# Two more chunk pairs of the first FFN in Strassen's form: the sixth of its third group and the fifth of its fourth

## The chip, the cores and the metric

The kernel runs on one core of one Trainium2 chip. The metric is the device time of one execution in microseconds. The median of three runs of the kernel before is 401.58 us (401.27 to 401.74).

## The reference

Four layers run one after another on one sequence of 2048 rows and 512 features, in bfloat16, each with a layer norm in front and a residual sum behind: linear attention A with 32 heads, gated FFN B with 1792 hidden features, then A and B again with the same weights.

```python
phi = lambda t: jnp.where(t > 0, t + 1, jnp.exp(t)) + 1e-6
kv = jnp.einsum("bhsd,bhse->bhde", phi(k), v)
num = jnp.einsum("bhqd,bhde->bhqe", phi(q), kv)
den = jnp.einsum("bhqd,bhd->bhq", phi(q), z)[..., None] + 1e-6     # z: phi(k) summed over s
A(x) = (num / den) @ wo                                            # q, k, v = x @ wqkv
B(x) = (silu(x @ w_gate) * (x @ w_up)) @ w_down
x = x + A(norm(x));  x = x + B(norm(x));  x = x + A(norm(x));  x = x + B(norm(x))
```

## The kernel before

**Layers and groups.** The layers are numbered 0 (A), 1 (B), 2 (A), 3 (B). The 2048 rows are 16 tiles of 128; the FFN works on four groups (0 to 3) of 512 rows. The 1792 hidden features are 14 chunks of 128 (0 to 13).

**Plain chunk.** A token such as `1u304` (layer 1, group 3, chunk 04) is eight matmuls of 512 columns on TensorE (PE): four with `Wg` into one bank, four with `Wu` into another. ScalarE (ACT) takes the silu of the first (`silu`, line 1013), VectorE (DVE) multiplies by the second and writes the chunk of `hT` (`h`, line 1018). Once layer 2's K and Q tiles have begun, ACT would have to change its table for a silu, so there the chunk is a tanh on ACT (line 1001) and two steps on DVE (`gst` line 1003, `h` line 1009).

**Strassen's form.** A token such as `1y243` (layer 1, group 2, pair 4, product 3) belongs to a family that computes chunks j and j + 7 of a group together. The two chunks, the two halves of the 512 features and the two halves of the group's rows make a 2 x 2 block product, done with seven products (Winograd's form of Strassen's algorithm) in place of eight. One product is four matmuls of 256 columns, two for the gate and two for the up projection, side by side in one bank. Function `gs` (line 1180) issues it and what follows it: products 1, 6 and 7 are copied by ACT into a buffer (`cp`, line 1248); after products 2, 3 and the later of 5 and 7, DVE adds the bank to such a buffer (`ca`, line 1227), ACT takes the silu (`sih`, line 1219), and GpSimd (POOL) or DVE multiplies into `hT` (`hp`, line 1242); after product 4, ACT takes a silu (line 1219) and DVE multiplies (`hh`, line 1258). Some products add into the bank of another one, and may only after that one was copied:

```python
own = FIRST[i]
fresh = own == i
...
assert done.issuperset({2: (1,), 6: (1,), 7: (6,), 4: (7,), 3: (5, 7)}.get(i, ()))
```

**Operands of the families.** Products 3, 5, 6 and 7 read sums of weight blocks (`ws`, line 1101). One piece of sums, `W0`, `W1`, `W2`, `W3`, serves two pairs: `W2` serves pairs 4 and 5. Layer 1 keeps `W2` in the first 4096 columns of the tensor `Wqkv`, whose own contents nobody needs between layers 0 and 2. Most products also read sums of blocks of the rows (`xs`, line 1147), one set for each group; group 3 keeps its set in `Wo`. Before layer 2 the attention's weights are loaded anew by POOL's queue, once all readers of the sums there are done (function `reload`, its loads through the helper `dma`, line 535): `R.ldk` and `R.ldk1` bring the K part in two halves of 256 KB, `R.ldq` and `R.ldv` the Q and V parts of 512 KB each, `R.ldo` brings `Wo`:

```python
for c in range(2):
    dma("pool", Wqkv[:, 2 * c:2 * c + 2, D:2 * D], wq3[:, 2 * c:2 * c + 2, D:2 * D], w=[f"Wk{c}"], kind="ldk")
dma("pool", Wqkv[:, :, 0:D], wq3[:, :, 0:D], w=["Wq"], kind="ldq")
dma("pool", Wqkv[:, :, 2 * D:], wq3[:, :, 2 * D:], w=["Wv"], kind="ldv")
```

**Other tokens.** `2k0` is a K tile of layer 2 (four matmuls of 512 columns, `phi` of it by ACT's exponential, line 700, and DVE), `2q10` a Q tile, `1p25` a piece of the down-projection of layer 1's group 2 (14 matmuls of 256 columns; it too is in Strassen's form).

**What sets the order.** It is written out by hand. The table `PROGRAM` lists the tokens in the order in which PE works; the list `PE_T` holds times that belong to it. The tables `ORDER["act"]`, `["dve"]`, `["pool"]`, `["sp"]` list every operation of the other engines by name (`1y243.hp` is the product of token `1y243`, `2x4.apply` a step of a tile's layer norm). Each engine runs its list in order; waits between engines follow from the buffers that an operation reads and writes. `ON_POOL` and `ON_ACT` hold the names of operations that are placed on another engine than the usual one. All matmuls of the tokens are issued by one helper (line 492).

Of the kernel before, what the change touches and what calls it, by code (L numbers as in the profile page):

```python
# [206 lines left out]
2d22 2d23 2g4 2d11 2d12 2g1 2d13 2q33 2v 2m0 2m1 2m3 2m2 2r1 2w3 2w2 2w0 2w1 2q30 2q32 2w4 2d31 2w6 2w8 2w7 2w10 2d33
2w9 2d30 2d32 2w11 2w5 3U008 3u008 3u001 3u004 3u010 3u000 2w12 3u005 3u009 3u002 2w15 3u012 2w13 3u011 2w14 3u007
3y101 3u003 3y105 3y111 3y106 3y115 3u006 3y116 3y102 3y107 3u013 3y104 3y103 3y121 3y112 3y117 3p01 3p05 3y113 3p06
3y125 3y114 3p02 3y131 3y126 3p07 3y132 3u106 3y136 3y122 3y127 3y137 3p03 3y151 3y124 3y135 3y152 3y156 3u113 3y157  # L210
3y123 3y155 3p04 3y133 3y141 3y154 3y134 3y211 3y145 3y146 3y153 3y255 3y216 3y215 3y147 3y142 3y217 3y212 3y251 3y144
# [1377 lines left out]
```

## Time and profile before

| what | value |
| --- | --- |
| median of three runs | 401.58 us (401.27 to 401.74) |
| the profiled execution | 401.14 us, of which the profile's span is 399.4 us |
| PE busy | 394.3 us, 2922 matmuls |
| DVE, ACT, POOL busy | 327.5, 268.8, 214.5 us |

The profile is one execution. The span is what the profiler sees from the first to the last instruction; 1.74 us of the execution lie around it. Busy time of an engine is the time in which an instruction of it ran; "idle before" gives what an engine waited for. In a timeline row, a start time and a duration stand first, then the engine, the line of the kernel, the operation, what it writes from what it reads, its shape and the number of equal instructions in a row; a duration covers them all, and since matmuls overlap at their ends, the next row's start tells better when the next one began. The names of tensors are those of the allocated buffers: `pk`, `Wqkv` or `Wo` as the operand of a matmul of 256 columns are mostly sums that are kept there.

### The profile page before, as it was taken

What the parts mean: (1) busy time and instruction counts of PE and PEld (TensorE: products, weight loads), DVE (VectorE), ACT (ScalarE), POOL (GpSimd) and SP (SyncE); (2) the same over time, 40 slices, a digit from 0 to 9 for tenths busy, and PEclk for the clock granted to TensorE, in tenths of its full rate; (3) what the DMA queues carried; (4) which work ended last, traced back from release to release, by engine and by line L of the source; (5) the groups of instructions that cost most, each with busy time, mean ns of one, the idle gap of its engine ahead of it and who ended that gap; (6) DMA issues with size and microseconds to landing.
All of it is one profiled execution on the core that took longest, in us unless ns stands there. A gap on an engine that the chain in (4) does not pass through costs nothing.

```text
span 399.4 us, 7922 instructions
## 1 busy us (share of the span) xinstructions
PE 394.3 (99%) x2922; PEld 264.5 (66%) x2922; DVE 327.5 (82%) x785; ACT 268.8 (67%) x569; POOL 214.5 (54%) x352
## 2 busy tenths in 40 slices
PE   7999999999999999999999999999999999999997
PEld 6444555445787787565786445454588888888886
DVE  5996599377987779699997666987698889899997
ACT  5999886763656876668367968695755673886550
POOL 5623254998879799960446503467747260431230
PEclk9999999999999999999999999999999999999999
DMA  8646662540020021721002103323112100100011
GB/s 268 167 91 228 158 158 60 150 121 2 2 42 12 2 41 29 210 50 45 2 16 59 33 15 67 69 53 67 39 28 41 36 19 2 55 0 2 2 53 54
DMA packets 53783, 25.43 MB, mean 64 GB/s; under 512 B 46512, under 2 KB 52144, under 8 KB 53744
## 3 DMA queue, kind: packets, MB, share of 16 engines
q1 hardware_dynamic: 51264, 16.27, 18.4%
q0 software_dynamic: 1936, 8.13, 6.4%
q10 hardware_dynamic: 544, 0.52, 0.4%
q8 instruction: 23, 0.38, 0.4%
q14 instruction: 16, 0.13, 0.1%
HBM read 11.80 MB, written 2.10 MB: 35 GB/s over the span
## 4 chain that ended last, share of the span: by engine, by line
PE 97%; DMA 1%; DVE 1%; ACT 0%; issue 0%; SPq 0%; DVEq 0%
PE pb L492 97%; DMA X<-in_A_x_dram 1%; DVE pq L1442 0%; PE pb L679 0%; ACT xnA L624 0%; ACT xnA L616 0%; DVE stats L609 0%; DVE etmp L809 0%; SPq L535 0%; DVEq L1559 0%; DVE xnA L655 0%; DVE mv L611 0%; DVE vpe L640 0%; DVE xnA L1368 0%
## 5 line engine op out<-in xcount | busy, mean ns | idle before, releaser
L492 PE MATMUL pb<-xnT,Wg 128*128 128x512 bf16 (+1 forms) x332 | 75.3, 334 | 0.0
L492 PE MATMUL pb<-xnT,Wu 128*128 128x512 bf16 (+1 forms) x332 | 75.3, 334 | 0.0
L1242 POOL TENSOR_TENSOR hT<-pq 128x256 bf16<-128x256 f32 x45 | 34.1, 769 | 45.4 <-ACT pq L1219 45.3
L1248 ACT ACTIVATE pq<-pb 128x512 f32<-128x512 f32 x63 | 36.6, 594 | 28.2 <-PE pb L492 24.8
L492 PEld LDWEIGHTS pb<-xnT,Wu 128*128 128x128 bf16 x332 | 32.5, 98 | 24.2
L1227 DVE TENSOR_TENSOR pq<-pb,pq 128x512 f32<-128x512 f32 x63 | 41.9, 682 | 5.7 <-PE pb L492 2.9
L492 PEld LDWEIGHTS pb<-xnT,Wg 128*128 128x128 bf16 x332 | 32.3, 98 | 21.2 <-DMA xnT<-xnB 0.2
L1018 DVE TENSOR_TENSOR hT<-tht,pb 128x512 bf16<-128x512 f32 x46 | 30.8, 681 | 17.2 <-ACT tht L1013 12.2
L644 POOL TENSOR_TENSOR rstd<-vpe,negh 128x1 f32<-128x1 f32 x62 | 36.5, 590 | 9.5 <-DVE vpe L640 7.3
L1013 ACT ACTIVATE tht<-pb 128x512 f32<-128x512 f32 x46 | 26.4, 594 | 22.5 <-PE pb L492 21.5
L492 PE MATMUL pb<-Wd,hT 128*128 128x256 bf16 x336 | 40.3, 273 | 0.0
L700 ACT ACTIVATE etmp<-pb 128x512 bf16<-128x512 f32 x64 | 36.7, 601 | 3.8 <-PE pb L492 2.9
L492 PEld LDWEIGHTS pb<-Wd,hT 128*128 128x128 bf16 x336 | 32.9, 98 | 4.2
L492 PE MATMUL pb<-pk,xnA 128*128 128x512 bf16 (+1 forms) x152 | 34.7, 362 | 0.0
L492 PE MATMUL pb<-xnT,Wqkv 128*128 128x512 bf16 (+1 forms) x132 | 32.8, 376 | 0.0
L705 DVE TENSOR_SCALAR etmp<-etmp 128x512 bf16<-128x512 bf16 x64 | 19.4, 314 | 15.5 <-ACT etmp L700 15.5
L492 PE MATMUL pb<-Wqkv,xnT 128*128 128x512 bf16 x128 | 30.8, 379 | 0.0
L1219 ACT ACTIVATE pq<-pq 128x256 f32<-128x256 f32 x63 | 24.9, 411 | 8.1 <-DVE pq L1227 8.0
L492 PE MATMUL pb<-GT,pq 128*128 128x512 bf16 x128 | 29.9, 379 | 0.0
L624 ACT ACTIVATE etmp<-X,sums 128x512 bf16<-128x512 bf16 x32 | 22.9, 715 | 5.0 <-DVE X L945 3.8
L628 POOL TENSOR_SCALAR mv<-sums 128x1 f32<-128x1 f32 x52 | 14.1, 275 | 21.2 <-DVE X L945 12.5
L945 DVE SCALAR_TENSOR_TENSOR X<-pb,X 128x512 bf16<-128x512 f32 x32 | 21.1, 681 | 3.5 <-PE pb L492 3.4
(218 smaller groups left out, 887.8 us busy)
## 6 DMA issues: line engine op xcount, KB each, us to landing
...
Wd<-in_B_w_down_dram POOLq DMA_DIRECT2D x7, 256.0 KB, 3.3
X<-in_A_x_dram SPq DMA_DIRECT2D x6, 256.0 KB, 4.8
Wqkv<-in_A_wqkv_dram SPq DMA_DIRECT2D x2, 512.0 KB, 7.4
Wo<-in_A_wo_dram POOLq DMA_DIRECT2D x2, 512.0 KB, 4.6
Wqkv<-in_A_wqkv_dram POOLq DMA_DIRECT2D x2, 512.0 KB, 5.1
```

The lines of the kernel that those rows point to most:

```text
L492: return op("pe", lambda e: e.matmul(o_ap, lhsT=lhsT, rhs=rhs, start=start, stop=stop, skip_group_check=skip), r=r, w=w, n=n)
L624: op("act", lambda a: a.activation(out=sq_ap, in_=X[:, t, :], func=ACT.Square, scale=-float(D), bias=sums[:, t:t + 1], accum_out=mv[:, t, ...
L644: op("pool", lambda p: p.tensor_tensor(out=rstd[:, t:t + 1], in0=vpe[:, t:t + 1], in1=negh[:], op=ALU.pow), r=[f"vp{t}", "negh"], w=[f"rs{ ...
L700: exps.append(op("act", lambda a: a.activation(out=etmp[e][:], in_=PB[pb], func=ACT.Exp), r=[f"pb{pb}"], w=[f"e{e}"], after=silus, kind="e ...
L705: op("dve", lambda v: v.tensor_scalar(out=etmp[e][:], in0=etmp[e][:], scalar1=1.0, scalar2=1e-6, op0=ALU.min, op1=ALU.add), r=[f"e{e}"], w ...
L945: op("dve", lambda v: v.scalar_tensor_tensor(out=X[:, t, :], in0=PB[pb], scalar=1.0, in1=X[:, t, :], op0=ALU.mult, op1=ALU.add, accum_out= ...
L1013: silus.append(op("act", lambda e: e.activation(out=tht[a][:], in_=PB[pg], func=ACT.Silu), r=[f"pb{pg}"], w=[f"th{a}"], after=exps, kind=" ...
L1018: op("dve", lambda v: v.tensor_tensor(out=hT[h][:, j, :], in0=tht[a][:], in1=PB[pu], op=ALU.mult), r=[f"pb{pu}", f"th{a}"], w=hk, kind="h")
L1219: silus.append(op("act", lambda e: e.activation(out=o_ap, in_=i_ap, func=ACT.Silu), r=r, w=w, after=exps, kind="sih" if len(w) == 1 else " ...
L1227: op("dve", lambda v: v.tensor_tensor(out=c, in0=PB[b], in1=c, op=ALU.add), r=[f"pb{b}", k], w=[k], kind="ca")
L1242: lambda e: e.tensor_tensor(out=hT[h][:, jj, o:o + 256], in0=c[:, 0:256], in1=c[:, 256:512], op=ALU.mult),
L1248: op("act", lambda e: e.activation(out=c, in_=PB[pb], func=ACT.Copy), r=pk_, w=[k], kind="cp")
```

## The change

Only tables change. Two plain pairs become families: chunks 5 and 12 of group 2 (`1u205`, `1u212`) become `1y251` to `1y257`, chunks 4 and 11 of group 3 (`1u304`, `1u311`) become `1y341` to `1y347`. Pairs 4 and 5 use the sums `W2`, and both groups have their sums of rows for other families, so no operation `ws` or `xs` is new. `PROGRAM` differs in these lines only (and in the wrapping of the lines behind):

```diff
-1u303 1y243 1u212 1u306 1u205 1u309 1y301 1y311 1u302 1y306 1u310 1y316 1y315 1y307 1y305 1u313 1y317 1y304 1y302
-1y312 1y303 1y313 1y314 2k0 2k1 2q10 2k4 1u304 2k3 2k2 2k6 1p21 2q01 2k5 1u305 1p26 1p22 1p27 1p25 1u311 1p24 1u312
+1u303 1y251 1y243 1y252 1y256 1y345 1u306 1y255 1y257 1y341 1u309 1y253 1y301 1y342 1y254 1y346 1y311 1u302 1y306
+1u310 1y347 1y315 1y316 1y344 1y307 1y343 1y305 1u313 1y317 1y304 1y302 1y312 1y303 1y313 1y314 2k0 2k1 2q10 2k4 2k3
+2k2 2k6 1p21 2q01 2k5 1u305 1p26 1p22 1p27 1p25 1p24 1u312 1p23 1p31 1p35 2k7 1p36 1p33 1p37 2k11 2q02 1p34 1p32 2q12
```

`PE_T` gets new numbers. The tables of ACT, DVE, POOL and SP get the operations of the new families in place of those of the four chunks, and in all four layers some neighbours change places. PE has 2946 matmuls in place of 2922, ACT 10 operations more, DVE 2, POOL 6, SP none. `ON_ACT` gets the name `1c303`, which moves nothing: the chunk's product stays on DVE, since the buffer that the other way needs is lent at that point. All lines behind the tables stand three lines lower (L492 becomes L495, L535 becomes L538, L1242 becomes L1245).

The first place is on PE, behind the chunk `1u303`, where layer 1's last chunks and families stand. Before:

```order
L492 MATMUL pb<-xnT,Wg 128x512 x4
L492 MATMUL pb<-xnT,Wu 128x512 x4
L492 MATMUL pb<-xnT,Wqkv 128x256 x4
L492 MATMUL pb<-xnT,Wg 128x512 x4
L492 MATMUL pb<-xnT,Wu 128x512 x4
L492 MATMUL pb<-xnT,Wg 128x512 x4
L492 MATMUL pb<-xnT,Wu 128x512 x4
L492 MATMUL pb<-xnT,Wg 128x512 x4
L492 MATMUL pb<-xnT,Wu 128x512 x4
```

The same place after:

```order
L495 MATMUL pb<-xnT,Wg 128x512 x4
L495 MATMUL pb<-xnT,Wu 128x512 x4
L495 MATMUL pb<-xnT,Wg 128x256 x2
L495 MATMUL pb<-xnT,Wu 128x256 x2
L495 MATMUL pb<-xnT,Wqkv 128x256 x4
L495 MATMUL pb<-xnT,Wg 128x256 x2
L495 MATMUL pb<-xnT,Wu 128x256 x2
L495 MATMUL pb<-pk,Wqkv 128x256 x4
L495 MATMUL pb<-Wo,Wqkv 128x256 x4
L495 MATMUL pb<-xnT,Wg 128x512 x4
L495 MATMUL pb<-xnT,Wu 128x512 x4
```

Behind `1u303` there stood `1y243` (the row with `Wqkv`, the last one there that reads `W2`) and three plain chunks; now there stand `1y251`, `1y243`, `1y252`, `1y256` and `1y345`, and the first plain chunk comes behind them.

The second place is on POOL, around the reload of the attention's weights. Before:

```order
L628 TENSOR_SCALAR mv<-sums 128x1
L1242 TENSOR_TENSOR hT<-pq 128x256
L535 DMA Wqkv<-in_A_wqkv_dram 128x2x512 x2
L628 TENSOR_SCALAR mv<-sums 128x1
L1242 TENSOR_TENSOR hT<-pq 128x256
L535 DMA Wqkv<-in_A_wqkv_dram 128x4x512 x2
L640 TENSOR_SCALAR vpe<-mv 128x1
L1242 TENSOR_TENSOR hT<-rrep 128x256
```

After:

```order
L1245 TENSOR_TENSOR hT<-pq 128x256 x2
L1150 TENSOR_TENSOR Wo<-xnT,Wo 128x512
L1245 TENSOR_TENSOR hT<-pq 128x256
L538 DMA Wqkv<-in_A_wqkv_dram 128x2x512 x2
L538 DMA Wqkv<-in_A_wqkv_dram 128x4x512 x2
L1245 TENSOR_TENSOR hT<-rrep 128x256
L538 DMA Wo<-in_A_wo_dram 128x4x512
L1245 TENSOR_TENSOR hT<-pq 128x256 x5
L1245 TENSOR_TENSOR hT<-GT 128x256
L768 TENSOR_TENSOR GT<-GT,pk 128x512
```

The four loads into `Wqkv` stood ahead of the layer norms of layer 2 (`mv`, `vpe`) and of four operations `xs` and `hp`; now they stand behind the last row sum of group 3 and directly ahead of the last products of layer 1 and of layer 2's first sums of K (`GT<-GT,pk`).

The third place is PE's start of layer 2, from the last two products of layer 1 (`1y313`, `1y314`) to the first piece of the down-projection, `1p21`. Before:

```order
L492 MATMUL pb<-Wo,Wg 128x256 x2
L492 MATMUL pb<-Wo,Wu 128x256 x2
L492 MATMUL pb<-Wqkv,xnT 128x512 x8
L492 MATMUL pb<-xnT,Wqkv 128x512 x4
L492 MATMUL pb<-Wqkv,xnT 128x512 x4
L492 MATMUL pb<-xnT,Wg 128x512 x4
L492 MATMUL pb<-xnT,Wu 128x512 x4
L492 MATMUL pb<-Wqkv,xnT 128x512 x12
L492 MATMUL pb<-Wd,hT 128x256 x14
```

After:

```order
L495 MATMUL pb<-Wo,Wg 128x256 x2
L495 MATMUL pb<-Wo,Wu 128x256 x2
L495 MATMUL pb<-Wqkv,xnT 128x512 x8
L495 MATMUL pb<-xnT,Wqkv 128x512 x4
L495 MATMUL pb<-Wqkv,xnT 128x512 x16
L495 MATMUL pb<-Wd,hT 128x256 x14
```

The chunk `1u304`, which stood between the K tiles `2k4` and `2k3`, is gone from there; its work stands ahead of `2k0` now.

## Rows read from the trace of the kernel before

**Rows 1.** The page: PE's busy time, granted clock by slice, the chain that ended last
```profile
PE 394.3 (99%) x2922; PEld 264.5 (66%) x2922; DVE 327.5 (82%) x785; ACT 268.8 (67%) x569; POOL 214.5 (54%) x352
...
PEclk9999999999999999999999999999999999999999
...
PE 97%; DMA 1%; DVE 1%; ACT 0%; issue 0%; SPq 0%; DVEq 0%
```

**Rows 2.** Waits of PE over the span: us in total, times, longest
```profile
PE pb L492 <- DVE hT L498: 1.2, 1, 1.2
PE pb L679 <- DVE xnA L655: 0.8, 1, 0.8
```

**Rows 3.** Timeline of PE, start and duration in us, from 152 to 194
```profile
152.80 1.04 PE L492 MATMUL pb<-pk,Wqkv 128*128 128x256 bf16 x8
...
154.15 0.39 PE L492 MATMUL pb<-pk,Wg 128*128 128x256 bf16 x2
...
156.13 1.03 PE L492 MATMUL pb<-xnT,Wg 128*128 128x512 bf16 x4
...
157.86 0.60 PE L492 MATMUL pb<-xnT,Wqkv 128*128 128x256 bf16 x4
...
166.07 1.03 PE L492 MATMUL pb<-xnT,Wg 128*128 128x512 bf16 x4
166.94 1.03 PE L492 MATMUL pb<-xnT,Wu 128*128 128x512 bf16 x4
167.80 0.60 PE L492 MATMUL pb<-Wo,pk 128*128 128x256 bf16 x4
...
176.49 1.89 PE L492 MATMUL pb<-Wqkv,xnT 128*128 128x512 bf16 x8
178.22 1.03 PE L492 MATMUL pb<-xnT,Wqkv 128*128 128x512 bf16 x4
...
190.77 3.22 PE L492 MATMUL pb<-Wd,hT 128*128 128x256 bf16 x28
193.83 1.69 PE L492 MATMUL pb<-Td,RT 128*128 128x256 bf16 x14
```

**Rows 4.** The page's groups of a family's side work: busy us, mean ns of one
```profile
L1242 POOL TENSOR_TENSOR hT<-pq 128x256 bf16<-128x256 f32 x45 | 34.1, 769 | 45.4 <-ACT pq L1219 45.3
L1248 ACT ACTIVATE pq<-pb 128x512 f32<-128x512 f32 x63 | 36.6, 594 | 28.2 <-PE pb L492 24.8
...
L1227 DVE TENSOR_TENSOR pq<-pb,pq 128x512 f32<-128x512 f32 x63 | 41.9, 682 | 5.7 <-PE pb L492 2.9
...
L1219 ACT ACTIVATE pq<-pq 128x256 f32<-128x256 f32 x63 | 24.9, 411 | 8.1 <-DVE pq L1227 8.0
```

**Rows 5.** Windows, 156 to 181: busy us of PE, weight loads, DVE, ACT, POOL
```profile
156.00:181.00 25.00, 25.00 (x148) 14.29 (x147) 19.73 (x40) 16.84 (x37) 19.72 (x31) 1.00 0.48 122
```

**Rows 6.** Waits of POOL, 156 to 212: us in total, times, longest
```profile
POOL GT L765 <- DVE pk L709: 11.2, 1, 11.2
```

**Rows 7.** Timeline of ACT: a copy (153.50) and the change of tables
```profile
153.50 0.60 ACT L1248 ACTIVATE rrep<-pb 128x512 f32<-128x512 f32 x1 [1.36 <-PE pb L492]
...
179.49 1.28 ACT L700 ACT_TABLE_LOAD   x1
180.78 0.60 ACT L700 ACTIVATE etmp<-pb 128x512 bf16<-128x512 f32 x1
```

**Rows 8.** Timeline of POOL: the issues of the four loads into `Wqkv`
```profile
158.76 1.53 POOL L535 DMA_DIRECT2D Wqkv<-in_A_wqkv_dram  x2 [0.23 <-PE pb L492]
...
161.18 1.56 POOL L535 DMA_DIRECT2D Wqkv<-in_A_wqkv_dram  x2
```

**Rows 9.** The page's DMA issues: KB each, median us from issue to landing
```profile
Wqkv<-in_A_wqkv_dram SPq DMA_DIRECT2D x2, 512.0 KB, 7.4
...
Wqkv<-in_A_wqkv_dram POOLq DMA_DIRECT2D x2, 512.0 KB, 5.1
...
Wqkv<-in_A_wqkv_dram POOLq DMA_DIRECT2D x2, 256.0 KB, 4.0
```

More of the change, by code (lines that the diff above doesn't have):

```diff
@@ L207 @@
[L207 to L211, printed above, removed]
@@ L218 @@
+3y323 3p27 3y367 3y362 3y333 3y364 3y324 3y363 3y341 3y345 3p24 3y346 3y342 3y334 3y347 3p23 3y344 3y343 3p31 3p32
+3p35 3p36 3p33 3p37 3p34
 """
@@ new lines @@
+0k11.id1 0q02.id1 0q02.exp 0k12.exp 0k12.id1 0q23.exp 0q22.id1 0q22.exp 0d0.ln 0d0.rex1 0d0.rex3 0q21.exp 0q10.id1
+0d0.rex 0q10.exp 0d0.rex2 0q20.exp 0d1.ln 0d1.rex3 i.c1 0d1.rex1 0G2.evac 0G3.evac 0d1.rex 0q30.exp 0d1.rex2 0q31.exp
+0M3.evac 0M0.evac 0M1.evac 0q33.exp 0d2.ln 0d2.rxs 0q33.id1 1x1.sq 1x2.sq 1x3.sq 1x2.apply 0q32.exp 1x0.sq 1x3.apply
+1x4.sq 1x5.sq 1x7.sq 1x6.sq 1x4.apply 1u012.silu 0d3.rep1 1u000.silu 1x9.sq 1x11.sq 1u001.silu 1x7.apply 1u007.silu
+0d3.rep 1u011.silu 1u004.silu 1u005.silu 0d3.rep3 1u006.silu 1u003.silu 1x6.apply 1x10.sq 1u010.silu 0d3.rep2
@@ new lines @@
+1u013.silu 1u002.silu 1y121.cp 1u008.silu 1u113.silu 1x8.sq 1y101.cp 1u009.silu 1u104.silu 1y122.sih 1y126.cp
+1u105.silu 1y106.cp 1x13.sq 1y127.cp 1y107.cp 1y131.cp 1y124.sih 1y136.cp 1x9.apply 1y102.sih 1y104.sih 1y137.cp
+1x12.sq 1y134.sih 1y123.sih 1y105.sih 1u112.silu 1y111.cp 1y116.cp 1x15.sq 1y127.sih 1y132.sih 1y117.cp 1y103.sih
+1y117.sih 1y112.sih 1x14.sq 1y135.sih 1y133.sih 1u111.silu 1y114.sih 1y221.cp 2x2.sq 1u106.silu 2x1.sq 1y226.cp
+1y201.cp 2x3.sq 1y227.cp 1y113.sih 2x0.sq 1u206.silu 1y222.sih 1y227.sih 1u213.silu 1y211.cp 1x13.apply 1y231.cp
@@ new lines @@
+2q31.id1 2q31.exp 2q21.exp 2q20.id1 2q03.exp 2q03.id1 2d0.ln 2d0.rex1 2d0.rex3 2d0.rex 2q13.exp 2d0.rex2 2q23.exp
+2q23.id1 2q22.exp 2q22.id1 2d2.ln 2d2.rex1 2d2.rex 2G2.evac 2G3.evac 2d1.ln 2q33.id1 2d1.rxs 2q33.exp 2M0.evac
+2M1.evac 2M2.evac 2d2.rex3 2d2.rex2 3x3.sq 3x2.sq 2q30.exp 3x0.sq 2q32.exp 3x1.sq 3x0.apply 3x8.sq 3x6.sq 3x4.sq
+3x9.sq 3x7.sq 3x6.apply 3x10.sq 2d3.rep 2d3.rep1 3u008.silu 3u004.silu 3x7.apply 3u010.silu 3u001.silu 2d3.rep2
+2d3.rep3 3u000.silu 3u009.silu 3u005.silu 3x5.sq 3x5.apply 3u012.silu 3x11.sq 3u002.silu 3x12.sq 3x15.sq 3u007.silu
@@ L263 @@
+3y307.sih 3y312.sih 3y357.sih 3y321.cp 3y303.sih 3y313.sih 3y361.cp 3y326.cp 3y336.cp 3y322.sih 3y327.cp 3y337.cp
+3y366.cp 3y332.sih 3y327.sih 3y367.cp 3y335.sih 3y367.sih 3y364.sih 3y324.sih 3y362.sih 3y323.sih 3y333.sih 3y341.cp
+3y363.sih 3y346.cp 3y347.cp 3y334.sih 3y342.sih 3y347.sih 3y344.sih 3y343.sih
 """,
```

265 lines of the change are left out of this document (126 added, 139 removed).

## The prediction

> **What bounds the kernel now.** I read the page first: TensorE (PE) is busy 394.3 of 399.4 us, its clock is granted in full in all 40 slices, and 97% of the chain that ended last is PE's matmul line [rows 1]. The view of PE's waits names little: 1.2 us once for an evacuation, 0.8 us once for a normalised input [rows 2], both far from the stretch that changes (156 to 212 us). PE runs without a hole there, so the kernel's time is the sum of its matmuls, and an edit is worth what it takes out of that sum less the waits that it puts in. Two prices are read from PE's timeline [rows 3]. A plain chunk is 8 matmuls of 512 columns: one ran from 166.07 to 167.80, 1.73 us. A run of 28 matmuls of 256 columns went from 190.77 to 193.83, 3.06 us, and 28 of that size is what one Strassen family of seven products issues.
>
> **What is taken out.** Two plain pairs, four chunks, go: 4 x 1.73 = 6.92 us, less rounding 6.90. Two families come: 2 x 3.06 = 6.12, or 6.10 where the row's own small gaps are left out. PE's sum falls by **0.80 us** (0.40 a pair), although it has 24 matmuls more (32 leave, 56 come). No sum of weights or of rows is added: those of pairs 4 and 5, and of both groups, stand for other families. 0.80 us is 0.2% of 401.58 us, and 0.2% is about what a measurement of this kernel can tell from no change, so the whole gain lies just on that edge.
>
> **Side work.** For each pair the families add to ScalarE (ACT) three copies and four silus, to VectorE (DVE) three sums and one product, to GpSimd (POOL) three products; the plain chunks' silus, tanhs and products go. By count that is ACT +10, DVE +2, POOL +6. From the mean durations of the groups (594, 682, 411 and 769 ns, [rows 4]; a plain chunk's silu and product, of the copy's and the sum's shape, taken at 594 and 682), the stretch before layer 2 gains on ACT 6 x 0.59 + 8 x 0.41 - 2 x 0.59 = 5.6 us, on DVE 6 x 0.68 + 2 x 0.41 - 2 x 0.68 = 3.5 us. It was 25 us long with ACT 16.84, DVE 19.73 and POOL 19.72 busy [rows 5] and becomes 27.65 long: 22.4, 23.2, and POOL up to 24.3. All fit under PE; POOL moreover leaves some of its six products (4.6 us) for the 11.2 us in which it waited for layer 2's first sums [rows 6]. I cost this at nothing as a sum of busy time; what can cost is order, below.
>
> **Copies that a product waits for.** Within a family a later product adds into a bank only after ACT has copied it. Row 152.80 (x8) starts with a seventh product; its copy runs on ACT from 153.50 for 0.60 [rows 7], and the fourth product, which needs it, starts at 154.15, 1.35 us after the seventh began. Three products back to back are 3 x 0.436 = 1.31. So the pattern "product, two other products, dependent one" holds PE for 0.04. The new families have it twice: 1y251, 1y243, 1y252, then 1y256; and 1y347, 1y315 with 1y316, then 1y344. Cost 2 x 0.04 = **0.09 us**; lower end 0; higher end 0.3 each, if ACT comes to the copy after another instruction of half a microsecond.
>
> **The reload of the attention's weights.** This is the part with the least room. The sums of weights for pairs 4 and 5 lie in a part of the QKV weights' own tensor, which POOL reloads once their last reader has run; layer 2's first matmuls read the reloaded tensor. Before, the last reader was 1y243, at 157.86; the first pair of loads started on POOL at 158.76 (0.90 after that), the second at 161.18 [rows 3, 8], and layer 2 began at 176.49, more than 10 us after they had landed. Now the new families read the same sums and the last reader is 1y343, and from its start to layer 2 PE has nine products, itself among them, and one plain chunk: 9 x 0.436 + 1.73 = 5.65 us.
> PE gets two families and loses only two chunks before layer 2 (the other two stood inside layer 2), so layer 2 starts at 176.49 + 6.10 - 3.45 = 179.1, its second half of the first K tile's operands is wanted at 179.5, and the first Q tile (178.22 before) at 180.86. 1y343 starts at 179.1 - 5.65 = 173.5. With the same 0.90, and 1.53/2 = 0.77 per issue on POOL [rows 8]: first K load 174.4, second 175.1, Q load 175.9. Landings by the page: 4.0 us for 256 KB, 5.1 for 512 KB from POOL [rows 9]. So K lands at 178.4 and 179.1 (0.7 and 0.4 us early), Q at 181.0 (0.15 late). The V load is wanted later still. Bounds: the Q load can be 0.15 early-to-late around zero, since it shared the DMA engines before with transposes and now stands in an emptier stretch; the high end is the slowest 512 KB of the page, 7.4 us, from the SP queue at the start [rows 9]. I take **0.08 us**, half of 0.15, since POOL's own rows are the nearest. Queued behind on POOL are the products 1y305.hp to 1y302.hp and the reload of Wo; PE's down-projection is the reader of the former and comes some 6 us later.
> The Trainium skill (DMA: Bandwidth & Descriptors, Anatomy of one DMA, the SWDGE path) states a fit of about 2.0 us plus bytes over 436 GB/s. Worked out from that page as an estimate, 256 KB would land in 2.6 us and 512 KB in 3.2, and the term would be zero with over a microsecond to spare; the rows (4.0 and 5.1) say otherwise here, and the sum goes by them.
>
> **The start of layer 2.** The change takes two chunks out of it: 1u304 stood among the K tiles, 1u311 among the down-projection. There ACT had switched to the table of the exponential (1.28 us from 179.49, first exponential at 180.78, [rows 7]) once its last silu had run. Now more silus stand before that switch, and layer 2 starts 2.65 us later, so I place the switch at about 182.7 and the first exponential at 184.0, 3.2 us after its matmuls ended instead of 2.6. PE goes on with K and Q tiles and a down-projection meanwhile; the first matmul that wants a bank back is 1u305, at about 188.4, and adding up the durations along DVE's order, I find what frees it done about half a microsecond before. In return DVE loses there two gated products of two steps each (2 x 2 x 0.68 = 2.7 us). I take zero; ends -0.2 and +0.8.
>
> **The rest of the tables.** The orders of ACT, DVE, POOL and SP are also permuted a little in all other layers, PE's is not. The waits that PE shows there are 2.2 us in all [rows 2], so a permutation can give at most a few tenths, and can take as much. I take zero, plus or minus 0.2.
>
> **Sum.** -0.80 + 0.09 + 0.08 = -0.63 us. The profiled execution took 401.14 us (span 399.4 and 1.74 around it): it would take 400.51. The median of the runs, 401.58, stands 0.44 above the profiled one, so I give **400.95**.
>
> **Rivals.**
> 1. *The whole gain, or a little more.* Neither thin place costs anything and the permuted tables close some of the tenths that PE waits elsewhere: 401.58 - 0.80 = 400.78, less 0 to 0.5, so 400.3 to 400.78. For it: the landings of before were taken with transposes in the same microseconds, and PE's waits outside the stretch leave something to win. Against it: the copy pattern is a row of before, and nothing was added to hide it.
> 2. *The reload lands late; slower.* One mechanism: layer 2's first K tile waits for the K loads. At the 7.4 us of the SP queue the first lands at 174.4 + 7.4 = 181.8, 2.65 us after PE wants it; the Q load's lateness lies under that. 401.58 - 0.80 + 0.09 + 2.65 = 403.5. It decides from a landing of 4.7 us on, and makes the kernel slower by over 0.2% from about 6.3 us. Against it: POOL's own loads of this size took 4.0 to 5.1.
> 3. *A backlog at the switch of tables.* ACT comes 0.5 to 1 us later to the first exponential than I place it, DVE with it, and PE waits for a bank at 1u305 or for a product at the down-projection: 401.2 to 401.9, no change that could be told; with two such waits 402.5.
> 4. *Matmuls are not priced by columns.* If a matmul of 256 columns cost more than half of one of 512, Strassen's form would lose. At a spacing of 98 ns for 256 columns and 131 for 512, a plain pair is 16 x 0.131 = 2.10 us and a family 28 x 0.098 = 2.74: +0.64 a pair, so 402.9. Those two figures are from the Trainium skill (TensorE: Matmul & The Clock Gate, Back-to-back issue gap), which gives 131 ns at 512 and 81 at 128 for a sustained stream; 98 is my interpolation, an estimate. The trace speaks against the mechanism: 1.73 us for 8 is 216 ns, and 3.06 for 28 is 109, a ratio of 1.98 [rows 3].
>
> **Chances.** My forecast (400.75 to 401.15): 0.42. Rival 1: 0.32. Small stalls of rivals 2 and 3 that leave it within 0.2% of before: 0.14. Rival 2 with the slower ending 0.06, rival 3 with it 0.04, rival 4 0.02. Faster is rival 1 and a sliver of the forecast, 0.35; slower 0.12; the same 0.53. Range 400.2 to 402.2: below lies little of rival 1, above the three slower cases.
>
> **What would show it.** Right: in the stretch from 156 to the start of layer 2 PE runs 2.65 us longer, 1p25 (193.83 before) starts 0.9 later than before, and what follows it, with 1u311 gone, 0.7 earlier; holes of about 0.04 ahead of 1y256 and 1y344. Wrong: a wait of PE for a DMA into the QKV weights, or the K loads landing more than 4.7 us after their issue (rival 2); a wait of the matmuls of 1u305 for DVE (rival 3); 28 products that take more than 3.1 us (rival 4); or PE's waits of 1.2 and 0.8 us elsewhere grown or gone, which the part on the rest of the tables puts at zero.

## The result, and the profile after

The changed kernel is slower: 405.09 us in the median of four runs (404.32 to 405.43), before 401.56 in the same runs. The ratio is 1.0086, with an interval of 1.0070 to 1.0102. The profiled execution took 405.43 us, its span 403.7 (before 401.14 and 399.4): 4.3 us more.

The page of the kernel after, where [rows 1] stood for before (busy time, clock by slice, chain that ended last):

```profile
PE 396.1 (98%) x2946; PEld 267.8 (66%) x2946; DVE 333.7 (83%) x787; ACT 271.9 (67%) x579; POOL 219.5 (54%) x358
...
PEclk9999999899999999999999999999999999999999
...
PE 93%; DVE 3%; issue 2%; DMA 1%; ACT 1%; POOL 0%; DVEq 0%; POOLq 0%
```

PE has 24 matmuls more and, which could not be if only the sum of matmuls had changed, more busy time; one slice, the eighth, has a lower clock; and DVE's share of the chain has risen from 1% to 3%. PE's waits of after, the answer to [rows 2]:

```profile
PE pb L495 <- DVE X L948: 3.0, 1, 3.0
PE pb L495 <- DVE hT L501: 1.2, 1, 1.2
PE pb L495 <- DMA xnT<-xnB: 0.2, 1, 0.2
```

One wait of 3.0 us for a residual sum of layer 0 (line 948) is new; the 0.8 us of before's second line, at the program's start, are not there. PE's timeline of after says where it stands: nearly 90 us ahead of the first matmul that the change touches.

```profile
70.47 1.03 PE L495 MATMUL pb<-xnT,Wu 128*128 128x512 bf16 x4
74.47 1.52 PE L495 MATMUL pb<-xnT,Wg 128*128 128x512 bf16 x4 [2.97 <-DVE X L948]
75.78 1.91 PE L495 MATMUL pb<-xnT,Wu 128*128 128x512 bf16 x4
77.49 1.43 PE L495 MATMUL pb<-xnT,Wg 128*128 128x512 bf16 x4
78.75 1.03 PE L495 MATMUL pb<-xnT,Wu 128*128 128x512 bf16 x4
```

The row at 74.47 is the plain chunk `1u007` of layer 1's first group. Behind the wait four matmuls take 1.71 us (75.78 to 77.49) in place of 0.86. The windows of after (PE, weight loads, DVE, ACT, POOL, then PE's granted clock) show why:

```profile
70.50:74.40 3.90, 1.00 (x5) 0.27 (x3) 3.90 (x4) 3.81 (x9) 3.89 (x4) 1.00 0.17 34
74.40:78.60 4.20, 4.13 (x12) 1.54 (x13) 2.65 (x8) 1.69 (x3) 4.00 (x9) 0.59 0.89 158
78.60:90.00 11.40, 11.40 (x55) 5.16 (x54) 5.52 (x8) 5.55 (x12) 8.36 (x14) 1.00 0.50 138
```

After three idle microseconds PE's granted clock was 0.59 for 4.2 us, most of it at the lower of its two levels (1.2 GHz), then full again. Beside before, PE stands 0.10 us later at the first chunk `1u012`, 3.23 later at `1u007` and 4.93 later at `1u011`: 3.13 for the wait and 1.70 for the clock.

What DVE and POOL did then, in that order:

```profile
67.72 0.95 DVE L887 RECIPROCAL rtok<-dsb 128x128 bf16<-128x128 f32 x1
69.24 4.56 DVE L658 TENSOR_SCALAR xnB<-X,mv,rstd 128x512 bf16<-128x512 bf16 x1 [0.57 <-POOL rstd L647]
73.72 0.68 DVE L948 SCALAR_TENSOR_TENSOR X<-pb,X 128x512 bf16<-128x512 f32 x1
```

```profile
68.63 0.57 POOL L647 TENSOR_TENSOR rstd<-vpe,negh 128x1 f32<-128x1 f32 x1
69.18 2.25 POOL L1104 TENSOR_TENSOR xnA<-Wg 128x512 bf16<-128x512 bf16 x2
71.40 1.14 POOL L1104 TENSOR_TENSOR pk<-Wu 128x512 bf16<-128x512 bf16 x1
72.51 1.14 POOL L1104 TENSOR_TENSOR xnA<-Wu 128x512 bf16<-128x512 bf16 x1
73.60 0.79 POOL L538 DMA_DIRECT2D Wd<-in_B_w_down_dram  x1
```

The DVE row at 69.24 is `1x5.apply`, the last step of a layer norm (tile 5 of layer 1): 0.41 us in the kernel before, here 4.56. It began 0.06 us after POOL began four sums of weights (`ws`) in a row, and ended 0.15 us after the last of them. That it began there is in the order itself: the step waits for `rstd`, and POOL makes `rstd` (68.63) in the instruction directly ahead of the four sums. The residual that PE waits for, `0w8.res`, stands behind the step on DVE. In the kernel before, these names stood in another order: POOL had one sum, then small steps and a DMA issue, and DVE had `0w8.res` seven places ahead of `1x5.apply`. The same step there, and POOL beside it:

```profile
69.68 0.41 DVE L655 TENSOR_SCALAR xnB<-X,mv,rstd 128x512 bf16<-128x512 bf16 x1
```

```profile
68.71 1.15 POOL L1101 TENSOR_TENSOR xnA<-Wg 128x512 bf16<-128x512 bf16 x1
69.83 0.34 POOL L628 TENSOR_SCALAR mv<-sums 128x1 f32<-128x1 f32 x1
```

It met only the last 0.18 us of one sum.

**The stretch that the change is about.** From `1u303` (161.06, 156.13 before) to the end PE needs 0.67 us less than before: 4.93 later there, 4.26 later at the last matmuls. Its start of layer 2, where [rows 3] had 176.49 and 178.22:

```profile
184.20 1.89 PE L495 MATMUL pb<-Wqkv,xnT 128*128 128x512 bf16 x8
185.93 1.03 PE L495 MATMUL pb<-xnT,Wqkv 128*128 128x512 bf16 x4
186.79 3.62 PE L495 MATMUL pb<-Wqkv,xnT 128*128 128x512 bf16 x16
```

Nothing waits there. The reload of the weights, where [rows 8, 9] stood, started at 179.44, 0.90 after 1y343, as the prediction had it; the landings (KB each, median us from issue to landing) are these:

```profile
Wqkv<-in_A_wqkv_dram POOLq DMA_DIRECT2D x2, 512.0 KB, 5.0
Wqkv<-in_A_wqkv_dram POOLq DMA_DIRECT2D x2, 256.0 KB, 3.3
```

### The profile page after: what moved, and what is told of

Same layout as the page of the kernel before. It is cut to its first block, busy times and chain, and to the rows that moved or that the text cites. A ratio compares the mean times of both kernels' runs of the same rounds, so it can differ in the third digit from the quotient of the medians.

```text
span 403.7 us, 7991 instructions
## 1 busy us (share of the span) xinstructions
PE 396.1 (98%) x2946; PEld 267.8 (66%) x2946; DVE 333.7 (83%) x787; ACT 271.9 (67%) x579; POOL 219.5 (54%) x358
## 4 chain that ended last, share of the span: by engine, by line
PE 93%; DVE 3%; issue 2%; DMA 1%; ACT 1%; POOL 0%; DVEq 0%; POOLq 0%
PE pb L495 92%; DMA xnT<-xnB 1%; DVE pq L936 1%; DVE X L948 1%; DVE pq L1445 0%; ACT GT L798 0%; DVE xnB L658 0%; ACT etmp L703 0%; POOL rstd L647 0%; PE pb L682 0%; DVE etmp L708 0%; DVE pq L918 0%; DVE etmp L812 0%; DVE xnT L690 0%; DVE pq L712 0%
## 5 line engine op out<-in xcount | busy, mean ns | idle before, releaser
L495 PE MATMUL pb<-xnT,Wg 128*128 128x512 bf16 (+1 forms) x324 | 73.7, 334 | 3.2 <-DVE X L948 3.0
L495 PE MATMUL pb<-xnT,Wu 128*128 128x512 bf16 (+1 forms) x324 | 73.6, 333 | 0.0
L1245 POOL TENSOR_TENSOR hT<-pq 128x256 bf16<-128x256 f32 x48 | 35.6, 752 | 47.4 <-ACT pq L1222 47.4
L1251 ACT ACTIVATE pq<-pb 128x512 f32<-128x512 f32 x66 | 38.7, 596 | 32.8 <-PE pb L495 27.9
L1230 DVE TENSOR_TENSOR pq<-pb,pq 128x512 f32<-128x512 f32 x66 | 44.3, 683 | 8.0 <-ACT pq L1251 4.5
L495 PEld LDWEIGHTS pb<-xnT,Wg 128*128 128x128 bf16 x324 | 31.7, 98 | 23.6 <-DVE X L948 3.5
L495 PEld LDWEIGHTS pb<-xnT,Wu 128*128 128x128 bf16 x324 | 31.9, 98 | 23.1 <-issue 1.1
L1021 DVE TENSOR_TENSOR hT<-tht,pb 128x512 bf16<-128x512 f32 x44 | 29.6, 682 | 17.2 <-PE pb L495 10.3
L495 PE MATMUL pb<-Wd,hT 128*128 128x256 bf16 x336 | 40.3, 273 | 0.0
L1016 ACT ACTIVATE tht<-pb 128x512 f32<-128x512 f32 x44 | 25.5, 594 | 15.8 <-PE pb L495 11.5
L495 PEld LDWEIGHTS pb<-Wd,hT 128*128 128x128 bf16 x336 | 32.9, 98 | 4.2
L495 PE MATMUL pb<-pk,xnA 128*128 128x512 bf16 (+1 forms) x152 | 34.7, 362 | 0.0
L495 PE MATMUL pb<-xnT,Wqkv 128*128 128x512 bf16 (+1 forms) x140 | 34.0, 370 | 0.0
L495 PE MATMUL pb<-Wqkv,xnT 128*128 128x512 bf16 x128 | 30.7, 379 | 0.1
L495 PE MATMUL pb<-GT,pq 128*128 128x512 bf16 x128 | 29.8, 379 | 0.0
```

Of the source, the lines that this page charges most:

```text
L495: return op("pe", lambda e: e.matmul(o_ap, lhsT=lhsT, rhs=rhs, start=start, stop=stop, skip_group_check=skip), r=r, w=w, n=n)
L1016: silus.append(op("act", lambda e: e.activation(out=tht[a][:], in_=PB[pg], func=ACT.Silu), r=[f"pb{pg}"], w=[f"th{a}"], after=exps, kind=" ...
L1021: op("dve", lambda v: v.tensor_tensor(out=hT[h][:, j, :], in0=tht[a][:], in1=PB[pu], op=ALU.mult), r=[f"pb{pu}", f"th{a}"], w=hk, kind="h")
L1230: op("dve", lambda v: v.tensor_tensor(out=c, in0=PB[b], in1=c, op=ALU.add), r=[f"pb{b}", k], w=[k], kind="ca")
L1245: lambda e: e.tensor_tensor(out=hT[h][:, jj, o:o + 256], in0=c[:, 0:256], in1=c[:, 256:512], op=ALU.mult),
L1251: op("act", lambda e: e.activation(out=c, in_=PB[pb], func=ACT.Copy), r=pk_, w=[k], kind="cp")
```

## The experiments

**Theories.** (1) The loss is the step `1x5.apply`, which cannot run while POOL runs sums back to back; the families themselves give what the stretch shows. (2) The families' side work costs, and the stall is its echo. (3) DVE's order alone, `0w8.res` behind `1x5.apply`, costs. Later a second question came up, of what then eats the families' gain; it is called theory 1b. In the diffs, ACT, DVE, POOL and SP stand for the lists of `ORDER`.

**e1_head: both families, the head's orders of before.** Of the four lists everything ahead of the changed stretch is taken from before (up to `1W2.ws3` on POOL, `1p14.rh` on DVE, `1y205.sih` or its neighbour on ACT, `2x7.xT` on SP); the places that matter:

```diff
 POOL
-Wd.ld2 1x4.nmr 1x5.pow 1W1.ws 1W1.ws2 1W0.ws6 1W1.ws4 Wd.ld
+Wd.ld2 1x4.nmr 1W1.ws 1x7.negm Wd.ld 1x7.pow 1W1.ws4 Wd.ld1
 DVE
-0w10.res 0w11.res 0d3.den 0w9.res 0d3.rcp 1x5.apply 0w8.res
+0w8.res 0w11.res 1x7.vpe 0w10.res 0d3.den 0d3.rcp 0w9.res 1x5.apply
```

> The changed kernel with the orders of ACT, DVE, POOL and SP of before up to the third group's sums (all that stands ahead of the changed stretch), and of after from there on. Theory 1 (the loss is one stall early in layer 1, where only neighbours in the tables changed places): PE's wait of 3.0 us at 74.5 us and the low clock behind it are gone, and what is left is the gain of the stretch, 0.63 us by the prediction's sum: 400.9 us, 0.5 to 0.8 under before. Theory 2 (the two families themselves cost): the time stays at 404 to 405. Theory 3 (the order on DVE alone is the cause): as theory 1 here.

Measured: 402.17 us in the median (401.54 to 403.23, 11 runs), ratio 1.0019 (1.0010 to 1.0028). The wait of 3.0 us and the low clock are gone, so theory 2 falls as the cause of the loss. But the gain is not there either: in the profiled execution (401.59 us) the stretch from `1u303` to the end costs as much as before (+0.04). PE's timeline of e1_head shows where the 0.7 went:

```profile
179.68 2.19 PE L495 MATMUL pb<-Wqkv,xnT 128*128 128x512 bf16 x8
182.12 1.02 PE L495 MATMUL pb<-xnT,Wqkv 128*128 128x512 bf16 x4 [0.25 <-DVE pq L1230]
```

The K tiles take 0.30 longer than after's 1.89, and the Q tile starts 0.25 behind their end, where in after it starts 0.16 ahead of it: 0.7 in all. The profile names DVE, which had long been done; the Q load was issued at about 176.45 (the four issues run from 174.92 for 3.04), and the two loads of that size landed after 5.8 us in the median (below), so at about 182.2, an estimate: PE waited for the load. The DMA view of e1_head from 174 to 183 us:

```profile
Wqkv<-in_A_wqkv_dram POOLq DMA_DIRECT2D x2, 512.0 KB, 5.8
Wqkv<-in_A_wqkv_dram POOLq DMA_DIRECT2D x2, 256.0 KB, 4.1
...
xnT<-xnA SPq DMA_TRANSPOSE x2, 4.7
```

Two of layer 2's transposes run beside the loads; in the kernel after, the same view lists none.

**e12_head_alone: the mirror.** The kernel before, without a new family, with after's orders in the head:

```diff
 POOL
-Wd.ld2 1x4.nmr 1W1.ws 1x7.negm Wd.ld 1x7.pow 1W1.ws4 Wd.ld1
+Wd.ld2 1x4.nmr 1x5.pow 1W1.ws 1W1.ws2 1W0.ws6 1W1.ws4 Wd.ld
 DVE
-0w8.res 0w11.res 1x7.vpe 0w10.res 0d3.den 0d3.rcp 0w9.res 1x5.apply
+0w10.res 0w11.res 0d3.den 0w9.res 0d3.rcp 1x5.apply 0w8.res
```

> The kernel before (no new family), with the changed kernel's orders of ACT, DVE, POOL and SP ahead of the changed stretch: the mirror of the first experiment. Theory 1: the whole loss is there without the change that the tables were made for: 1x5.apply takes 4.5 us, PE waits 3.0 us at 1u007 and its clock falls behind that in some runs, 404.5 to 406.5. Theory 2 (the families cost): 401.5.

Measured: 406.05 us (405.47 to 406.98), ratio 1.0109 (1.0093 to 1.0124). The wait (PE's waits of e12_head_alone) and the long step (its DVE timeline) are there in full:

```profile
PE pb L492 <- DVE X L945: 3.0, 1, 3.0
```

```profile
69.56 4.56 DVE L655 TENSOR_SCALAR xnB<-X,mv,rstd 128x512 bf16<-128x512 bf16 x1 [0.48 <-POOL rstd L644]
```

Behind the wait the granted clock is 0.60 for 4.3 us. So the whole loss is there without the change that the tables were made for: 4.57 us over before in the same runs, where after lost 3.53.

**e4_before_chain: four sums in a row in the kernel before.** Only POOL's list changes:

```diff
-1W1.ws 1x7.negm Wd.ld 1x7.pow 1W1.ws4 Wd.ld1 1W0.ws6 1W1.ws2 1W0.ws
+1W1.ws 1W1.ws2 1W0.ws6 1W1.ws4 1x7.negm Wd.ld 1x7.pow Wd.ld1 1W0.ws
```

> The kernel before, where on POOL the same four sums of weights stand back to back, as after has them (three of them moved up next to the first; nothing on DVE moves). Theory 1: the step 1x5.apply, 0.41 us before, starts beside the run of sums and ends when it ends, at about 73.2 us: 3 to 3.7 us long; the products behind it come 1 to 1.5 us later and PE waits up to 1 us: 401.6 to 403. If the long step has a cause in the changed part, it stays at 0.41 us and the time at 401.6.

Measured: 402.20 us (401.82 to 402.56), ratio 1.0016 (1.0007 to 1.0025). DVE's row and POOL's last sum and its next step, from the timelines of e4_before_chain:

```profile
69.72 3.66 DVE L655 TENSOR_SCALAR xnB<-X,mv,rstd 128x512 bf16<-128x512 bf16 x1
```

```profile
72.08 1.14 POOL L1101 TENSOR_TENSOR xnA<-Wu 128x512 bf16<-128x512 bf16 x1
73.21 0.25 POOL L628 TENSOR_SCALAR mv<-sums 128x1 f32<-128x1 f32 x1
```

From 0.41 to 3.66 us by POOL's order alone, ending 0.16 behind the last sum; PE waits 0.6 us for a product behind it. As theory 1 had it; the time is 0.8 us over before in the same runs. The residual ahead of the step (line 945, reading a bank) ran from 69.17 for 0.63 beside the first sum: it is not every DVE instruction that is kept out.

**e3_dve_swap: only DVE's order mended in after.**

```diff
-0d3.rcp 1x5.apply 0w8.res 1u000.h
+0d3.rcp 0w8.res 1x5.apply 1u000.h
```

> The changed kernel, where on DVE the residual 0w8.res is moved ahead of the step 1x5.apply; POOL's order stays with its four sums in a row. Theory 1: the step is still kept out until POOL's run ends at about 73.6 us (3.5 us or more), PE no longer waits for 0w8.res at 1u007, but the products 1u000.h, 1u012.h, 1u001.h behind the step come 2 to 3 us later than before, and PE waits 1 to 2 us for their banks one chunk later: 402.0 to 404. Theory 3 (DVE's order is the whole cause): 400.8 to 401.3.

Measured: 402.95 us (402.40 to 403.89), ratio 1.0038 (1.0025 to 1.0052). The step takes 4.56 us as before the edit. PE no longer waits for the residual but 1.0 us for a product, at 75.04, and its clock does not fall there (1.00 in the windows up to 78.6). So DVE's order decides what PE waits for and how long, but the step stays long without it, and theory 3 falls as the whole cause. The loss needs both orders: POOL's four sums make the step long, which costs PE a wait of 0.6 (e4_before_chain) or 1.0 us, and `0w8.res` behind the step makes 3.0 of it, with the low clock after it.

**e5_chain2: a DMA issue in the middle of the four sums.**

```diff
-1x5.pow 1W1.ws 1W1.ws2 1W0.ws6 1W1.ws4 Wd.ld
+1x5.pow 1W1.ws 1W1.ws2 Wd.ld 1W0.ws6 1W1.ws4
```

> The changed kernel, where on POOL the DMA issue Wd.ld stands in the middle of the four sums of weights, two on either side. Theory 1 (DVE's step 1x5.apply is kept out as long as POOL's instructions follow each other, and gets in at the DMA issue): the step takes about 2.3 us, half of the 4.56 it took behind four sums. If it were kept out by one sum only, 1.1 us; if by something other than POOL's run, 4.5 us as before.

Measured: 405.27 us, a single execution, so only its rows are used. The step takes 3.03 us, from 70.20 to 73.22, and PE waits 1.4 us for the residual behind it (a second wait, of 1.5 us at 85, is of the kind that e2_dma_first shows next). Two sums are 2.25 long, and the DMA issue (72.34 for 0.79) is in it too; the step got in behind that. So the length follows POOL's run, as theory 1 says, but my 2.3 left out that an issue can keep DVE out as well.

**e2_dma_first: the DMA issue ahead of the four sums.**

```diff
-1x5.pow 1W1.ws 1W1.ws2 1W0.ws6 1W1.ws4 Wd.ld
+1x5.pow Wd.ld 1W1.ws 1W1.ws2 1W0.ws6 1W1.ws4
```

> The changed kernel, where on POOL one DMA issue (the load Wd.ld) is moved from behind the four sums of weights to ahead of them; nothing else moves, DVE's order least of all. Theory 1 (DVE's layer norm step 1x5.apply is kept out for as long as POOL runs sums back to back, because POOL began 0.06 us earlier): the step now starts beside a DMA issue, takes 0.4 to 0.6 us in place of 4.56, PE's wait of 3.0 us is gone, and the time is 400.8 to 401.3. Theory 3 (the order on DVE, with 0w8.res behind the step, costs in itself): most of the wait stays, 403 to 405. If DMA traffic made the step slow, the step stays long, since the load only starts earlier.

Half a miss. The step falls from 4.56 to 0.80 (69.31 to 70.11, the issue runs from 69.23 to 70.02), and PE does not wait at 74. But the time did not come back: 404.27 us in the median, with runs between 400.94 and 407.02, ratio 1.0052 (1.0025 to 1.0079). In the profiled execution (406.33) the next place of the same kind took over, ten microseconds later (DVE first, then POOL, then PE of e2_dma_first):

```profile
80.16 3.38 DVE L591 TENSOR_TENSOR Td<-Wd 128x512 bf16<-128x512 bf16 x1
```

```profile
79.66 0.77 POOL L538 DMA_DIRECT2D Wd<-in_B_w_down_dram  x1
80.45 1.16 POOL L1104 TENSOR_TENSOR pk<-Wg 128x512 bf16<-128x512 bf16 x1
81.56 0.58 POOL L647 TENSOR_TENSOR rstd<-vpe,negh 128x1 f32<-128x1 f32 x1
82.11 1.14 POOL L1104 TENSOR_TENSOR pk<-Wu 128x512 bf16<-128x512 bf16 x1
```

```profile
84.20 1.04 PE L495 MATMUL pb<-xnT,Wu 128*128 128x512 bf16 x4 [2.86 <-DVE hT L1021]
```

This DVE step has two inputs in SBUF and came 0.50 us into a DMA issue; it ended 0.29 behind the second sum. The same DVE row took 1.95 us in the profiled execution of after; another row of its kind took 0.42 beside no sum (75.03 here). That the quickest run of this kernel, 400.94, is under every run of before fits an execution in which neither place is hit; that execution was not profiled.

**e6_p21_first: e1_head with more work ahead of layer 2.** One token moves in `PROGRAM`:

```diff
-1y314 2k0 2k1 2q10 2k4 2k3 2k2 2k6 1p21 2q01
+1y314 1p21 2k0 2k1 2q10 2k4 2k3 2k2 2k6 2q01
```

> The kernel of the first experiment (the head's orders of before, both families), where on PE one piece of layer 1's down-projection, 1p21 (14 matmuls, 1.53 us), stands ahead of layer 2's first K tile in place of behind the seven tiles; nothing else moves. It gives the reload of the attention's weights 1.53 us more. Theory 1b (what the first experiment lost against the sum, about 1.4 us in the median, is the K and Q loads landing after PE wants them, by an amount that differs from run to run): 400.6 to 401.1, with a spread of half a microsecond or so like before's. Rival (the families' side work on ACT, DVE and POOL costs, or jitter elsewhere): the median stays at 401.8 to 402.5 with a spread of 1.5 us.

Measured: 401.25 us (400.53 to 401.94), ratio 0.9989 (0.9980 to 0.9998): a little faster than before, 0.9 better than e1_head, with a median just above the expected range. The spread was 1.4 us, where half a microsecond was expected. In its profiled execution (401.48) the K tiles no longer wait, but the Q tile still does, 0.60 us, and now the profile names the load:

```profile
183.54 1.02 PE L495 MATMUL pb<-xnT,Wqkv 128*128 128x512 bf16 x4 [0.60 <-DMA Wqkv<-in_A_wqkv_dram]
```

Its DMA view from 174.5 to 184 us says why 1.53 us more room was not enough:

```profile
Wqkv<-in_A_wqkv_dram POOLq DMA_DIRECT2D x2, 512.0 KB, 7.4
...
xnT<-xnA SPq DMA_TRANSPOSE x2, 4.4
```

The two loads of 512 KB, Q and V, landed after 7.4 us in the median, against 5.0 in after; two transposes ran beside them, as in e1_head.

**e8_pair25 and e9_pair34: one family each.** The two chunks of the other pair are plain again, where they stood before (e8_pair25 without `1y341` to `1y347`, e9_pair34 without `1y251` to `1y257`):

```diff
 e8_pair25
-1y345 1y341 1y342 1y346 1y347 1y344 1y343
+1u304 1u311
 e9_pair34
-1y251 1y252 1y256 1y255 1y257 1y253 1y254
+1u212 1u205
```

> The head's orders of before, and of the two families only the sixth pair of the third group; chunks 4 and 11 of the fourth group are plain again, where they stood in before. The last reader of the sums W2 is then 1y253, about 9 us earlier, so the reload has more than 8 us to spare. Theory 1b: half of the gain is kept, 0.40 us: 400.9 to 401.2, narrow spread. Rival (a family's side work costs more than its matmuls save): at or above before, 401.4 or more.

> The head's orders of before, and of the two families only the fifth pair of the fourth group; chunks 5 and 12 of the third group are plain again, where they stood in before. The last reader of the sums W2 is still 1y343, 5.65 us ahead of layer 2. Theory 1b: the late loads eat the gain of 0.40 us and more in many runs: 401.3 to 402.3, spread above 1 us. Rival (each family costs by its side work): about the same as with the other pair alone.

e8_pair25 took 407.18 us (406.76 to 407.91) and answers nothing on the family: my premise was wrong. The last reader was done at 164.9, but POOL reaches the loads only at 173.29, since they stand behind the row sums and products in its list; PE gets to layer 2 sooner with a family less, and waits 0.97 for the second half of the first K tile's weights. The tanh that I put back on ACT stands ahead of the first exponential there, and PE waits a further 1.11 for ACT. In all its stretch costs 5.57 us more than before. e9_pair34 took 403.48 (401.92 to 406.44). Its profiled execution (402.23) waits 1.2 us for the Q load, and its stretch costs 1.07 more than before: the wait eats more than the family gives, as expected, but the runs go higher than expected, and what happened in those over 405 was not profiled.

**e10_head_sp and e11_sp_p21: after's order on SP.** Both start from e1_head and take the whole SP list of after, in which the transposes `2x0.xT` and `2x2.xT` stand earlier; e11_sp_p21 also has 1p21 ahead of layer 2:

```diff
-1x12.xT 1x15.xT 2x1.xT 2x3.xT 2x4.xT 2x0.xT 2x5.xT 2x6.xT 2x2.xT 2x7.xT
+1x15.xT 1x12.xT 2x0.xT 2x1.xT 2x2.xT 2x3.xT 2x4.xT 2x5.xT 2x6.xT 2x7.xT
```

> The kernel of the first experiment (both families; ACT, DVE and POOL with the head's orders of before), but with the changed kernel's whole order on SP. The first experiment had taken before's order of layer 2's transposes with it, so that six of them ran at 168 to 176 us and two of these beside the reload of the weights; the changed kernel runs four there and the last is done before the reload starts. Theory 1b (the first experiment lost the gain because the loads ran beside transposes and landed up to 0.8 us later): no transpose in the reload's window, K loads land in 3.3 us and the Q load in 5.0 to 5.5, PE waits at most 0.2 us there, median 400.7 to 401.1. Rival (side work of the families): 402.2 as in the first experiment.

> The kernel of e10_head_sp, with the piece 1p21 of the down-projection ahead of layer 2's first K tile on PE, which gives the reload 1.53 us more. Theory 1b: no wait for a load into the QKV weights in any run, so the narrow spread of before and the whole of the stretch's gain: 400.5 to 400.9. If the reload is not what makes runs differ, it is no better than e10_head_sp.

403.15 us (402.86 to 403.40) and 402.90 (402.53 to 403.56). Both miss, for a reason of the mixing: after's SP order, with before's on DVE, makes PE wait 1.6 us once, near 123 us, for a sum of `hT`. Behind that they answer: no transpose runs beside the loads, and the 512 KB loads land after 5.5 and 5.6 us; e10_head_sp loses 0.46 at the Q tile all the same, and its stretch gains only 0.07; e11_sp_p21 waits for no load, and its stretch gains 0.68.

**e13_early_p21: the two edits at the reload, without that.** e6_p21_first with two transposes moved on SP:

```diff
-2x1.xT 2x3.xT 2x4.xT 2x0.xT 2x5.xT 2x6.xT 2x2.xT 2x7.xT
+2x1.xT 2x0.xT 2x3.xT 2x2.xT 2x4.xT 2x5.xT 2x6.xT 2x7.xT
```

> The kernel of the first experiment (both families, the head's orders of before) with two edits at the reload: on SP the transposes 2x0.xT and 2x2.xT stand behind 2x1.xT and 2x3.xT in place of behind 2x4.xT and 2x6.xT, so that they are done before the reload; on PE the piece 1p21 stands ahead of layer 2's first K tile. Theory (the loss was the stall in the head, and what then stands between the families and their gain is only the wait for the Q load): no wait at 1u007 and none at the first Q tile, the whole 0.67 us of the stretch is kept, 400.6 to 401.0, 0.1 to 0.2% under before. If the Q load still lands late, 401.2 as with 1p21 alone.

Measured: 401.19 us (400.41 to 402.58, 11 runs), before 401.49, ratio 0.9990 (0.9980 to 1.0001): 3.9 under the changed kernel, and against before just not told apart. The median misses the expected 400.6 to 401.0 and stands where e6_p21_first stood, so the runs do not show that the transposes' move gains time; the profiled execution does show what it does there. In it (401.09) the 512 KB loads land after 5.1 us, PE waits for nothing between 156 and 200, and the whole stretch gains 0.68:

```profile
179.84 1.69 PE L495 MATMUL pb<-Wd,hT 128*128 128x256 bf16 x14
181.37 1.89 PE L495 MATMUL pb<-Wqkv,xnT 128*128 128x512 bf16 x8
183.09 1.03 PE L495 MATMUL pb<-xnT,Wqkv 128*128 128x512 bf16 x4
```

What it lacks of the 0.68 in this execution came before 70 us, where it ran 0.57 behind the profiled execution of before. Such small differences ahead of 70 us are in other executions too (0.01 to 0.57 at `1u303`, where no stall had been), and their cause stays open.

**One table.** From PE's timelines, the start of `1u303` less before's 156.13; the time from there to the Q tile `2q10` (less 1.53 where 1p21 stands in between); and what PE gains or loses from `1u303` to the last piece of the down-projection, 3p34. The families put 2.77 into the second column and take 0.68 out of the third if nothing waits. In seven of the traces the record of the first matmul of `1u303` is missing; there its start is taken 0.22 ahead of the next one's. e8_pair25 and e9_pair34, with one family, are left out.

| kernel | `1u303` later by | `1u303` to `2q10` | `1u303` to the end |
| --- | --- | --- | --- |
| before | 0 | 22.09 | 0 |
| e4_before_chain | 0.81 | 22.10 | +0.01 |
| e12_head_alone | 5.72 | 22.10 | +0.02 |
| after | 4.93 | 24.87 | -0.67 |
| e11_sp_p21 | 2.06 | 24.87 | -0.68 |
| e13_early_p21 | 0.57 | 24.86 | -0.68 |
| e5_chain2 | 4.37 | 25.29 | -0.25 |
| e3_dve_swap | 1.61 | 25.31 | -0.24 |
| e10_head_sp | 2.22 | 25.33 | -0.07 |
| e2_dma_first | 5.16 | 25.51 | +0.03 |
| e1_head | 0.40 | 25.59 | +0.04 |
| e6_p21_first | 0.25 | 25.63 | +0.08 |

The first column is the head's, the second the reload's, and the third, with both families, is -0.68 plus what the second has over 24.87 (within 0.15). So the two losses are separate: the head costs 4.93 in after, and the loads cost between nothing and 0.76 us by how they land. In after's own profiled execution the loads were quick.

**The landings sort by the transposes.** The 512 KB loads took 5.0 to 5.7 us in the profiled executions of the seven kernels whose transposes were done before them (after, e2_dma_first, e3_dve_swap, e5_chain2, e10_head_sp, e11_sp_p21, e13_early_p21), and 5.8, 7.4, 6.5 and 6.5 in the four with transposes beside them (e1_head, e6_p21_first, e8_pair25, e9_pair34). The 256 KB loads took 3.3 to 3.5 us in the former and 3.6 to 4.9 in the latter. These are medians of two loads in one execution each; e13_early_p21 differs from e6_p21_first by the place of the two transposes alone (7.4 there, 5.1 here).

## Why the prediction was wrong

The forecast was 400.95 us, the median is 405.09.

**The step that failed** is the one on the rest of the tables: "a permutation can give at most a few tenths, and can take as much. I take zero, plus or minus 0.2." No run contradicts the first half. The second does not follow: what a permutation can take is not bounded by the waits that PE shows now (and of the 2.2 us that the step names, [rows 2] show 2.0; a third wait has the rest). It took 4.93 us at the one place. The sign that the prediction set for this step, one of PE's two old waits grown or gone, pointed elsewhere too: what came was a wait of 3.0 us that had not been there. The step looked at PE's waits alone, took every instruction of the other engines at its usual duration and set no engine's list beside another's, and so could not see an instruction that takes eleven times its usual one because of its neighbour on another engine.

**The row stood in the trace of before.** The same step of another tile, on DVE, and what POOL did beside it:

```profile
166.03 1.23 DVE L655 TENSOR_SCALAR xnA<-X,mv,rstd 128x512 bf16<-128x512 bf16 x1 [1.24 <-POOL rstd L644]
```

```profile
165.96 1.16 POOL L1147 TENSOR_TENSOR Wo<-xnT,Wo 128x512 bf16<-128x512 bf16 x1
```

1.23 us in place of 0.41, from 0.07 behind POOL's start to 0.14 behind its end. There it cost PE nothing, so I passed over it. It has the same sign too: the step waited for `rstd`, and POOL went on at once. With it in hand, the order of after, where four sums of 1.14 us stand directly behind that `rstd`, would have asked for 4.6 us.

The Trainium skill (SBUF — State Buffer, Who interferes with whom) says that VectorE and GpSimd share a pair of ports to SBUF; a VectorE `tensor_scalar` in its two-port modes contends with GpSimd for it, and an instruction with two inputs in SBUF does with a GpSimd instruction that reads SBUF; whoever starts first keeps it for the whole instruction, and the other is fully blocked. This case's rows agree so far as they go (1.23 for the step beside one POOL instruction that started first, 3.38 for the step with two inputs in SBUF; an instruction that reads a bank ran beside a sum at its 0.63), and go further: behind four POOL instructions in a row the wait was not one instruction but all four (4.56). That it is this port, and that the step ran in such a mode, is the Trainium skill's reading, which no row shows; the runs show that the length follows POOL's run.

**The clock.** Its term was zero as well. The fall from 1.00 to 0.59 behind 3.0 us of idle PE made 1.70 of the 4.93 in the profiled execution. Two of after's four runs have a mean clock of 1.000 and took 404.32 and 404.76; the two with 0.996 took 405.42 and 405.43. So the fall does not come in every run, and part of the loss differs from run to run; without it, the 3.13 us of the wait less the families' 0.67 are still a loss of 2.5.

**The families' price** was right: -0.80 for the matmuls. The two places of the copies waited 0.04 and 0.07 in after (foreseen 0.04 each), so the stretch should give -0.69, and gave -0.67 where nothing else waited. The side work cost PE nothing there, as foreseen.

**The reload** was the right place, with the right matmul, but the term was mis-sized. I took 0.08 us from POOL's median landings; in the profiled executions with both families it ranged from 0 (after) to 0.76 (e6_p21_first, although it has 1.53 us more room). That after's execution stands near the forecast here is partly luck: its 5.0 us is the quickest landing of all. Mostly the Q load lands late, as [rows 9] let expect, and the K loads only in e1_head; what I did not weigh is that the loads of this size differ by up to 2.4 us between executions (5.0 to 7.4, the longest with transposes beside them), so that the high end counted oftener than the middle. The 7.4 us that I had as the high end came true in e6_p21_first.

**The switch of tables** took nothing in after, as I had it: PE waits neither at 1u305 nor in the down-projection.

**The rivals.** Of the slower ones, the mechanism of the second, loads that land late, is real, but mostly at the Q tile and not at the K tile where it was priced: with both families the K loads took 3.3 to 4.1 us, under the 4.7 from which that rival decides (4.9 in e8_pair25, where PE waited 0.97 for one). It cost nothing in after's profiled execution and 1.2 us at most in an experiment with the loads where after has them, not 2.65, and did not decide; the third and fourth did not occur. None of them stood where the time was lost, since all looked at the changed lines.
